# Batch 3's up product by Strassen's scheme, with joins on VectorE and copies on ScalarE

## The chip, the core and the metric

The kernel runs on one core of a Trainium2 chip. The metric is the time of one execution on the device, in microseconds (us). PE is the tensor engine, PEld its weight load, DVE the vector engine, ACT the scalar engine, POOL GpSimd, SP the engine that issues most of the transfers.

## What is computed

Attention with a few global and a window of local keys, then a low-rank mix over the sequence and a channel MLP with residual:

```python
# q, k, v: (4, 8, 768, 64); U: (768, 32); V: (32, 768); w_ch1: (512, 2048); w_ch2: (2048, 512)
scores = q @ k.T / 8 + bias            # 8 global keys, 96 local ones, a slope for each head
a = softmax(where(keep, scores, -1e9))
x = (a @ v) -> (4, 768, 512)           # heads side by side
h = x.T @ U @ V
u = x + h.T
out = u + relu(u @ w_ch1) @ w_ch2      # float32
```

`u @ w_ch1` is called the up product here, the product with `w_ch2` the down product.

## The kernel before, in words

The work is cut into 16 pairs of heads; pair i is heads 2(i % 4) and 2(i % 4) + 1 of batch i // 4. For each pair q and k are loaded and cast to fp16, transposed (by PE, from pair 7 on by transposing transfers, `turn`, L295), scored in `visit` (L352), scaled with the bias on DVE (`st_S`, L364), exponentiated on ACT (`st_E`, L376), multiplied with v (`st_av`, L383) and normed on DVE (`st_norm`, L403). POOL casts the result to fp16 (`st_x16`, L415). The low-rank mix follows: `st_low` and `st_lt` (L428, L439; L419 for some pairs), `st_M3` (L448), whose result DVE adds to the fp32 x (`st_add`, L461, two instructions of 128x384). Then `st_C` (L499) casts the sum to fp16 on POOL, and `st_X` (L492) issues a transposing transfer on SP that writes a quarter of uT, the transposed u of the batch. Four such quarters make a batch's uT; the up product of a batch waits for pair 3, 7, 11 or 15 last.

The up product (`up_mm`, L512) makes one 128-row block of the hidden layer in a PSUM bank with four matmuls over the 512 channels. Its moving side is a group of tokens: 384 and 384 for batches 0 and 1, 512 and 256 for batches 2 and 3 (`TG`, L65). So batches 2 and 3 have 16 blocks of four 512-column matmuls and 16 of four 256-column ones each. ACT takes each block out with a ReLU (`up_relu`, L526) into one of two tiles, htr0 and htr1.

The down product of batches 0 and 1 is plain (`down_mm`, L529). That of batches 2 and 3 goes by Strassen's scheme in Winograd's form, two row blocks of 128 tokens at a time (a row pair): seven products of eight 256-column matmuls (`product`, L595) in the order 1, 5, 6, 2, 7, 4, 3 (`PRODUCTS`). Three PSUM banks A, B, C serve a row pair. Product 1 opens A, 6, 7 and 4 add to it; between them DVE takes the value of A out (`gather`, L611, "a" after product 1, "b" after 6, "c" after 7) and joins it with B and C to the four quarters of the output. The sums that the products 5, 6, 7, 3 need on the hidden side are four DVE instructions for a row pair, `h_sum` (L572), those on the weight side are made once (`w_sum`, L561).

The whole order is written down by a planner inside the kernel (L630 to the end). Each piece of work is a `Step` (L643) with its engine or a choice of engines, a cost in us, the steps it depends on, the number of PSUM banks it needs, and sometimes a due time (`pace(i)`, L729) or laziness. The planner keeps a clock for each engine and for the DMA bus, and issues the step that can start first. At each turn PE takes the first of these that is ready: an attention step, a plain down product, a Strassen product (`next_product`, L993; between up groups at the rate of `PACE`, L1039), an up group (`do_up`, L944). The instructions of an engine then run in exactly this order, each waiting for its own semaphores, so a step that comes later than the planner thought holds up all that stands behind it on its engine. `open_pair` (L956) makes the steps of one row pair when the up groups of its tokens are put.

Staging tiles are in rotating pools: `stp` (loaded q, k, v and their fp16 form), `kp`, `scp` (scores), `vap`, `xp` (x, fp16 x, uT), `ffp` (hidden and output). The h sums before lie in free slots of `stp` and `scp`, and every second output block in one of `stp`.

Of the kernel before, what the change touches and what calls it, by code (L numbers as in the profile page):

```python
# [11 lines left out]
FP32 = mybir.dt.float32  # L12
# [8 lines left out]
def kernel(  # L21
# [13 lines left out]
    nc = tc.nc  # L35
# [35 lines left out]
    stp = ctx.enter_context(tc.tile_pool(name="stp", bufs=2))  # L71
    kp = ctx.enter_context(tc.tile_pool(name="kp", bufs=2))
    scp = ctx.enter_context(tc.tile_pool(name="scp", bufs=2))
    vap = ctx.enter_context(tc.tile_pool(name="vap", bufs=2))
    xp = ctx.enter_context(tc.tile_pool(name="xp", bufs=2))
    ffp = ctx.enter_context(tc.tile_pool(name="ffp", bufs=2))
    psum = ctx.enter_context(tc.tile_pool(name="psum", bufs=1, space=bass.MemoryType.PSUM))

    banks = [psum.tile([P, 512], FP32, name=f"bank{j}") for j in range(8)]
# [381 lines left out]
    def st_add(i, g):  # L461
# [99 lines left out]
    def w_sum(k, part):  # L561
        cs = slice(part * HC // 2, (part + 1) * HC // 2)
        o, x, y = (t[:, cs] for t in WSUM[k])
        nc.vector.tensor_tensor(o, x, y, ALU.subtract)

    sums, accs = {}, {}

    def quarters(b, n):
        g, ts = group(b, n)
        return htrs[b, g][:, 0:HC, ts], htrs[b, g][:, HC:NJC, ts]  # L570

    def h_sum(b, n, k):  # L572
        if k in (1, 3):
            if n // 2 % 2 == 0:
                nm = "qst" if k == 1 else "kst"
                home = [
                    stp.tile([P, 2, NSB, D], FP32, name=nm, tag=nm, bufs=2)
                    .rearrange("p h n d -> p (h n d)").bitcast(FP16)[:, 0:HC * P]
                    for _ in range(2)
                ]  # L580
            else:
                nm = f"sp{k // 2}"
                t = scp.tile([P, W], FP32, name=nm, tag=nm, bufs=1).bitcast(FP16)
                home = [t[:, j * HC * P:(j + 1) * HC * P] for j in range(2)]
            for j in range(2):
                sums[b, n, (1, 2, 3, 4)[k - 1 + j]] = home[j].rearrange("p (c t) -> p c t", c=HC)
# [6 lines left out]
        nc.vector.tensor_tensor(S[k], x, y, op)  # L593

    def product(b, n, k):  # L595
        (a11, a12), (a21, a22) = quarters(b, n), quarters(b, n + 1)
# [8 lines left out]
        for c in range(HC):  # L605
# [2 lines left out]
                skip_group_check=not fresh,  # L608
            )

    def gather(b, n, k):  # L611
        acc, t, cs, fresh = {
            "a": ("A", n, lo, True), "b": ("A", n, hi_, True), "c": ("A", n + 1, hi_, True),
            "11": ("B", n, lo, False), "12": ("C", n, hi_, False), "22": ("C", n + 1, hi_, False),
            "21": ("A", n + 1, lo, True),
        }[k]
        if (b, t) not in osbs:
            if t == n:
                osbs[b, t] = ffp.tile([P, DM], FP32, name="osb", tag="osb", bufs=3)
            else:  # L620
                osbs[b, t] = stp.tile([P, 2 * NSB, D], FP32, name="vst", tag="vst", bufs=2).rearrange(
                    "p n d -> p (n d)")[:, 0:DM]
# [215 lines left out]
    def pair(i):  # L838
# [36 lines left out]
        else:  # L875
# [4 lines left out]
            free_of[u][0].first = lc  # L880
        m = add(("m3", i), "PE", 0.34, lambda: st_M3(i), [("tc", i)], banks=2)
        free_of[m] = [
            add(("add", i, g), "DVE", 0.55, lambda g=g: st_add(i, g), [("m3", i)])
            for g in range(2)
        ]
# [18 lines left out]
    for st in pe_todo + waiting:  # L904
# [8 lines left out]
    since, last_out = 0, deque()  # L913
    left = {(b, g): TG[b][g] for b in range(B) for g in range(2)}
    relus, prods, opened, wsums = {}, [], [], {}

# [38 lines left out]

    def open_pair(b, n):  # L956
        g = int(n >= TG[b][0])
        rel = [relus[b, g, j] for j in range(NJC)]
        before = opened[-2] if len(opened) > 1 else None
        homes = [before[k] for k in PRODUCTS] if before else [  # L960
            steps[k, NPAIR - 1, j] for k in ("cq", "e") for j in range(2)]
        stored = before["end"] if before else [steps["cv", NPAIR - 1]]
        me = {}
        for k, deps in ((3, rel), (1, rel), (2, []), (4, [])):
            me["S", k] = other("DVE", 0.7, lambda k=k: h_sum(b, n, k), deps + homes + [
                me["S", j] for j in {2: (1,), 4: (3, 2)}.get(k, ())])
        for k in PRODUCTS:
            me[k] = Step("PE", 0.872, lambda k=k: product(b, n, k), rel, banks=int(k in "125"))
            me[k].nm = ("Q", b, n, k)
        for k, src in ("a", "1"), ("b", "6"), ("c", "7"), ("21", "4"), ("11", "2"), ("22", "5"), ("12", "3"):  # L970
            me["G", k] = other("DVE", 0.43, lambda k=k: gather(b, n, k), [me[src]] + stored)
# [17 lines left out]
        me["free"] = {"1": [me["G", "21"]], "5": [me["G", "12"]], "2": [me["G", "11"]]}  # L989
        opened.append(me)  # L990
        prods.append((b, n, me, list(PRODUCTS)))

    def next_product(now):  # L993
        for b, n, me, todo in sorted(prods[:2], key=lambda p: 0 if ups_q else -len(p[3])):
# [22 lines left out]
    def do_down():  # L1017
        if not begun:
            b, n = downs_q.popleft()
            parts = [  # L1020
                Step("PE", 0.87 if b or j else 1.08, lambda j=j: down_mm(b, n, j), banks=(j == 0))
                for j in range(NJC // 4)
            ]
            for p in parts:
                p.nm = ("D", b, n)
            ev = other("DVE", 0.65, lambda: down_add(b, n), parts[-1:] + list(last_out)[:1])
            if len(last_out) == 3:
                last_out.popleft()
            last_out.append(other("SP", 0.55, lambda: down_out(b, n), [ev], move=0.8))
            begun.extend(parts)  # L1030
            left[b, int(n >= TG[b][0])] -= 1
            put(begun.popleft(), [ev])
        else:
            put(begun.popleft())
            if not begun and not downs_q:
                sum_weights((2, 3))

    UP, RELU = 0.2165, 0.0865
    PACE = {(2, 1): 1, (3, 0): 2, (3, 1): 2}  # L1039
    begun, after, filled, lately = deque(), 0, 0, 0  # L1040
    while pe_todo or ups_q or downs_q or begun or prods:
        now = clock["PE"]
        drain(now)
        room = free_banks()[0][0]
# [5 lines left out]
        if not (after and down <= now):  # L1050
# [1 line left out]
                p for p in pe_todo if p.start() <= now + 0.05  # L1052
                and (p.banks != 2 or now < 31 or free_banks()[2][0] <= now + 0.5)
            ), None)
        prod = next_product(now)
        if step is not None:
            pe_todo.remove(step)
            put(step, free_of.get(step, ()))
# [1 line left out]
        elif down <= now + 0.05 and (begun or since >= 5 or after or up > now):  # L1060
            since = since if begun else max(0, since - 5)
            do_down()
            after = max(0, after - 1)
        elif prod and (lately >= PACE[ups_q[0][:2]] if up <= now + 0.05 else True):
            do_product(*prod)
            lately = 0
        elif up <= now + 0.05:
            b, g, _ = ups_q[0]
            do_up()
            since, after, lately = since + UP * TG[b][g] / 0.65, 0, lately + 1  # L1070
        else:
            soon = [p.start() for p in pe_todo + waiting] + [up, down]
            soon += [me[k].start() for _, _, me, todo in prods[:2] for k in todo]
            clock["PE"] = max(min(soon), now + 0.05)
            if 8 < now < 30 and clock["PE"] < math.inf:
                filled += 0.8 * (clock["PE"] - now) / 0.056
# [42 lines left out]
```

## Time and profile before

| | us |
|---|---|
| runs (3) | 224.8, 225.51, 226.29; median 225.51 |
| the profiled execution's own time | 225.93 |
| span of its profile | 223.0 |
| PE busy | 217.3 |
| DVE, ACT, POOL busy | 154.3, 115.0, 83.4 |

The page gives busy times of the engines, 40 slices of the span with the busy share in tenths, the chain of work that ended last (each step followed back to what released it), and groups of instructions by line. "PE 92%" in the chain means that for 92% of the span the end was set by PE's own work. In groups and timelines a PE instruction has its pipeline's fill in it, so that a row of eight 256-column matmuls shows 1.04 us and is followed by the next row 0.87 us after its start.

### The profile page before, as it was taken

To read this page: it belongs to the slowest core of one execution; us is meant where nothing else is said; L and a number is where in the kernel's file an instruction comes from. 1 tells how busy PE (TensorE), PEld (TensorE's weight loads), DVE (VectorE), ACT (ScalarE), POOL (GpSimd) and SP (SyncE) were. 2 spreads that over 40 slices of the span, in tenths; PEclk is the share of its full clock that TensorE was granted. 3 is DMA by queue.
4 is the path that set the end of the run, shared out by engine and by line. 5 is a ranking of instruction groups with operands and counts; after the bars stand their busy time and mean duration, and the time that the engine had idled before them with its cause. 6 is when DMAs were issued, how large, how long until landed. Compare 5 with 4: busy or idle time off the path is not lost.

```text
span 223.0 us, 5373 instructions
## 1 busy us (share of the span) xinstructions
PE 217.3 (97%) x2144; PEld 143.9 (65%) x2147; DVE 154.3 (69%) x349; ACT 115.0 (52%) x201; POOL 83.4 (37%) x125
## 2 busy tenths in 40 slices
PE   7999999999999998999999999999999999999994
PEld 3665876666565555655566555556988656688883
DVE  5768739576779595979977798797876702274662
ACT  5788576986464026664487040969224244444100
POOL 6646795605635653382624726322210000000000
PEclk9999999999999999999999999999999999999999
DMA  6999999999889998979799999710110400200204
GB/s 183 317 324 203 318 229 252 215 197 215 194 227 196 246 241 180 233 148 240 155 215 172 222 178 257 160 38 0 38 35 3 188 0 3 94 0 3 94 24 165
DMA packets 88871, 35.69 MB, mean 160 GB/s; under 512 B 78320, under 2 KB 85520, under 8 KB 88848
## 3 DMA queue, kind: packets, MB, share of 16 engines
q1 hardware_dynamic: 84320, 31.07, 59.1%
q0 software_dynamic: 4528, 4.29, 11.8%
q8 instruction: 16, 0.26, 0.5%
q14 instruction: 7, 0.06, 0.1%
HBM read 27.46 MB, written 6.29 MB: 151 GB/s over the span
## 4 chain that ended last, share of the span: by engine, by line
PE 92%; DMA 4%; DVE 2%; issue 1%; POOL 0%; DVEq 0%; POOLq 0%
PE bank L519 37%; PE bank L539 17%; PE bank L606 16%; PE bank L359 4%; PE bank L393 3%; PE bank L234 3%; DMA uT<-x 2%; PE bank L389 2%; PE bank L316 2%; PE bank L323 2%; PE bank L454 2%; PE bank L152 2%; DMA qst<-in_q_dram 1%; PE bank L431 1%; PE bank L423 1%; PE bank L478 1%
## 5 line engine op out<-in xcount | busy, mean ns | idle before, releaser
L519 PE MATMUL bank<-uT,w 128*128 128x384 f16 (+2 forms) x512 | 92.9, 326 | 0.8 <-DMA uT<-x 0.8
L527 ACT ACTIVATE htr<-bank 128x384 f16<-128x384 f32 (+2 forms) x128 | 60.1, 491 | 56.0 <-PE bank L519 53.4
L519 PEld LDWEIGHTS <-w 128*128 128x128 f16 x512 | 47.9, 98 | 28.3 <-issue 1.0
L378 ACT ACTIVATE ep<-sp 128x1408 f16<-128x1408 f32 x24 | 33.0, 1373 | 26.5 <-DVE sp L370 26.1
L539 PE MATMUL bank<-w,htr 128*128 128x512 f16 x192 | 45.8, 379 | 0.0
L370 DVE SCALAR_TENSOR_TENSOR sp<-bank,relcat 128x512 f32<-128x512 f32 (+1 forms) x72 | 41.2, 637 | 3.5 <-PE bank L359 3.3
L539 PEld LDWEIGHTS <-htr 128*128 128x128 f16 x192 | 17.5, 98 | 17.9
L417 POOL CAST x<-x_sb 128x384 f16<-128x384 f32 x30 | 17.2, 577 | 31.1 <-DVE x_sb L413 31.1
L127 POOL CAST v<-vst 128x768 f16<-128x768 f32 x16 | 13.8, 864 | 19.1 <-DMA vst<-in_v_dram 17.4
L501 POOL CAST x<-x_sb 128x768 f16<-128x768 f32 x12 | 10.3, 861 | 19.3 <-DVE x_sb L464 15.4
L413 DVE TENSOR_TENSOR x_sb<-bank,rcp 128x384 f32<-128x384 f32 x30 | 16.7, 558 | 1.0
L606 PEld LDWEIGHTS <-htr 128*128 128x128 f16 x144 | 14.0, 98 | 2.2
L393 PE MATMUL bank<-v,ep 128*128 128x65 f16 x192 | 15.5, 193 | 0.0
L393 PEld LDWEIGHTS <-ep 128*128 128x128 f16 x192 | 13.6, 98 | 2.3
L464 DVE TENSOR_TENSOR x_sb<-bank,x_sb 128x384 f32<-128x384 f32 x24 | 12.3, 552 | 3.6 <-PE bank L454 2.5
L389 PE MATMUL bank<-vA,ep 128*128 128x65 f16 x160 | 13.8, 194 | 0.0
L343 ACT ACTIVATE ep<-bank 128x512 f16<-128x512 f32 (+1 forms) x24 | 11.7, 576 | 2.4 <-PE bank L323 1.4
L406 DVE RECIPROCAL rcp<-bank 128x6 f32<-128x6 f32 x32 | 6.1, 191 | 9.2 <-PE bank L393 8.6
L606 PE MATMUL bank<-w,htr 128*128 128x256 f16 x96 | 12.1, 273 | 0.0
L389 PEld LDWEIGHTS <-ep 128*128 128x128 f16 x160 | 10.9, 97 | 1.8
L284 POOL COPY vA<-v 128x650 f16<-128x650 f16 x16 | 11.7, 731 | 0.9
L624 DVE TENSOR_TENSOR osb<-bank,x_sb 128x256 f32<-128x256 f32 x12 | 5.1, 422 | 9.5 <-PE bank L606 9.5
(109 smaller groups left out, 292.9 us busy)
## 6 DMA issues: line engine op xcount, KB each, us to landing
qst<-in_q_dram SPq DMA_DIRECT2D x16, 384.0 KB, 5.5
kst<-in_k_dram SPq DMA_DIRECT2D x16, 384.0 KB, 5.8
vst<-in_v_dram SPq DMA_DIRECT2D x16, 384.0 KB, 5.4
out_dram<-osb SPq DMA_DIRECT2D x17, 256.0 KB, 2.7
w<-in_moe_w_ch_dram POOLq DMA_DIRECT2D x6, 512.0 KB, 10.2
out_dram<-vst SPq DMA_DIRECT2D x5, 256.0 KB, 2.0
w<-in_moe_w_ch_dram POOLq DMA_DIRECT2D x1, 1024.0 KB, 10.7
out_dram<-osb SPq DMA_DIRECT2D x2, 128.0 KB, 1.7
```

The lines of the kernel that those rows point to most:

```text
L127: nc.gpsimd.tensor_copy(vt.rearrange("p n h d -> p h n d")[:, :, :, 0:D], vsts.pop(i).rearrange("p (h n) d -> p h n d", h=2),)
L370: nc.vector.scalar_tensor_tensor(out=sps[i, hi][:, c0:c0 + tot], in0=raw.pop((i, hi, c))[:, 0:tot], scalar=qk_scale / slope[2 * (i % NP) + ...
L378: nc.scalar.activation(ep, sps.pop((i, hi)), AF.Exp, scale=slope[2 * (i % NP) + hi])
L389: nc.tensor.matmul(ob[:, qi], ep[:, OF[qi - 1]:OF[qi - 1] + P], vA[:, qi - 1, hi], start=True, stop=False,)
L393: nc.tensor.matmul(ob[:, qi], ep[:, DG[qi]:DG[qi] + P], vt[:, qi, hi], start=(qi == 0), stop=True,)
L413: nc.vector.tensor_tensor(xo, ob[:, :, 0:D], rb, ALU.mult)
L417: nc.gpsimd.tensor_copy(x16, xo)
L464: nc.vector.tensor_tensor(dst, ups3.pop((i, g))[:, 0:GT].rearrange("p (t d) -> p t d", t=NTG), dst, ALU.add)
L519: nc.tensor.matmul(hps[:, 0:cols], w1_16[:, dc, jt * P:(jt + 1) * P], uTs[b][:, dc, c0:c0 + cols], start=(dc == 0), stop=(dc == NDC - 1),)
L527: nc.scalar.activation(htrs[b, g][:, jt], hps_t.pop((b, g, jt))[:, 0:TG[b][g] * P], AF.Relu)
L539: nc.tensor.matmul(cps, htr[:, jc, ts], w2_16[:, jc], start=(b > 0 and jc == 0), stop=(jc == NJC - 1),)
L606: nc.tensor.matmul(accs[b, n, acc], x[:, c], y[:, c], start=(fresh and c == 0), stop=(c == HC - 1), skip_group_check=not fresh,)
```

## The change

The up product of batch 3 is no longer made by `up_mm`. It goes by Strassen's scheme over the whole batch: w_ch1 and uT are quartered (256 channels by 1024 hidden rows, 256 channels by 384 tokens), and for each of 8 hidden blocks j seven products of two 384-column matmuls are made, 56 products in all. Where the scheme takes a value of bank A out, ACT copies it into an SBUF tile ("cut"), DVE joins it with bank B or C into the tile `hidden` (fp16), ACT takes the last quarter out with a ReLU, and the other three quarters get their ReLU in SBUF, on ACT or POOL. At most two blocks j are open at a time. The weight sums (8 instructions of 128x1024) and the four sums of u may go to DVE or POOL, and so may the h sums of the down product; the planner decided for POOL in all weight sums and 11 of 24 h sums. For these tiles the attention's pools (`stp`, `kp`, `scp`, `vap`) are closed after the last pair and a new pool `last` takes their memory; the h sums of batch 2 therefore begin only then.

For pairs 7 and 15, DVE writes the fp16 x itself (`st_add16`, two instructions, out of PSUM and the fp32 x), before the two adds that update the fp32 x, and the transfer `st_X` waits for these two. POOL's cast `st_C` is left out for them.

The planner's loop gets the new products (`next_quad`, at most six in a row while another product or up group is ready), and with other steps its order moves elsewhere too: in the stretch of batch 1's up product the visits of pairs 8 to 11 and their low-rank steps stand at other places, and around the end of attention batch 2's down products come later. The total of PE's other work is the same.

The core of the diff:

```diff
+    def st_add16(i, g):
+        b, dc = i // NP, i % NP
+        ts = slice(NTG * g, NTG * (g + 1))
+        nc.vector.tensor_tensor(
+            x16s[b][:, dc, ts], ups3[i, g][:, 0:GT].rearrange("p (t d) -> p t d", t=NTG),
+            xs[b][:, ts, dc * P:(dc + 1) * P], ALU.add,
+        )
...
-        nc.vector.tensor_tensor(S[k], x, y, op)
+        eng.tensor_tensor(S[k], x, y, op)
...
+    def up_product(j, k):
+        b11, b12, b21, b22 = u_quarters()
+        x, y, acc, fresh = {
+            "1": (a11w, b11, "A", True), "2": (a12w, b21, "B", True),
+            "3": (upw.get(4), b22, "C", False), "4": (a22w, usum.get(4), "A", False),
+            "5": (upw.get(1), usum.get(1), "C", True), "6": (upw.get(2), usum.get(2), "A", False),
+            "7": (upw.get(3), usum.get(3), "A", False),
+        }[k]
+        if fresh:
+            qacc[j, acc] = bank()[:, 0:GT]
+        for c in range(2):
+            nc.tensor.matmul(
+                qacc[j, acc], x[:, c, j * P:(j + 1) * P], y[:, c], start=(fresh and c == 0),
+                stop=(c == 1), skip_group_check=not fresh,
+            )
+
+    def up_cut(j, k):
+        cuts[j, k] = last_pool().tile([P, GT], FP32, name=f"cut{k}", tag=f"cut{k}", bufs=2)
+        nc.scalar.copy(cuts[j, k], qacc[j, "A"])
+
+    def up_join(j, k):
+        acc, cut, row, cs = {
+            "11": ("B", "a", j, slice(0, GT)), "12": ("C", "b", j, slice(GT, S)),
+            "22": ("C", "c", j + HC, slice(GT, S)),
+        }[k]
+        nc.vector.tensor_tensor(late["h"][:, row, cs], qacc[j, acc], cuts.pop((j, cut)), ALU.add)
+
+    def up_last(j):
+        nc.scalar.activation(late["h"][:, j + HC, 0:GT], qacc[j, "A"], AF.Relu)
+
+    def up_floor(j, k, eng):
+        t = late["h"][:, j] if k == "11" else late["h"][:, j + HC, GT:S]
+        if eng is nc.scalar:
+            eng.activation(t, t, AF.Relu)
+        else:
+            eng.tensor_scalar_max(t, t, 0.0)
...
+        if i in (NPE - 1, NPAIR - 1):
+            halves = [("half", i, g) for g in range(2)]
+            for g in range(2):
+                add(halves[g], "DVE", 0.55, lambda g=g: st_add16(i, g), [("m3", i)])
+            add(("xt", i), "SP", 1.2, lambda: st_X(i), halves + [("read", b - 2)], move=0.3)
+            return
...
-        (b, g, jt) for b in range(B) for lo in range(0, NJC, 4 if b == 0 else NJC)
+        (b, g, jt) for b in range(B - 1) for lo in range(0, NJC, 4 if b == 0 else NJC)
...
-            me["S", k] = other("DVE", 0.7, lambda k=k: h_sum(b, n, k), deps + homes + [
+            me["S", k] = other(SUM, 0, lambda e, k=k: h_sum(b, n, k, e), deps + homes + [
...
+    RATIO = 6
+    SUM = (("DVE", 0.7), ("POOL", 2.3))
+    gone = [steps["n", i, hi] for i in (NPAIR - 2, NPAIR - 1) for hi in range(2)]
...
+    def sum_up_weights():
+        for k in (1, 2, 4, 3):
+            for part in range(2):
+                deps = [last_add[0]] + (gone if k == 3 else [])
+                deps += [sumsof["w", j, part] for j in {2: (1,), 4: (2,)}.get(k, ())]
+                sumsof["w", k, part] = other(
+                    SUM, 0, lambda e, k=k, part=part: up_w_sum(k, part, e), deps, lazy=0.8)
...
-        prod = next_product(now)
+        prod, quad = next_product(now), next_quad(now)
...
+        elif quad and not (mixed >= RATIO and (prod or up <= now + 0.05)):
+            do_quad(*quad)
+            mixed += 1
```

In the changed kernel the lines are: `st_add16` L481, `st_add` L474, `w_sum` L582, `h_sum` L607, `product` L620, `up_w_sum` L645, `u_sum` L659, `up_product` L672, `up_cut` L679, `up_join` L686, `up_last` L689, `up_floor` L694 and L696, `gather` L712, `up_mm` L537.

More of the change, by code (lines that the diff above doesn't have):

```diff
@@ L559, with w_sum, h_sum @@
             (T4, wB[:, :, lo], T2), (T3, wB[:, :, hi_], wA[:, :, hi_])]
-    def w_sum(k, part):
+    def w_sum(k, part, eng=nc.vector):
         cs = slice(part * HC // 2, (part + 1) * HC // 2)
         o, x, y = (t[:, cs] for t in WSUM[k])
-        nc.vector.tensor_tensor(o, x, y, ALU.subtract)
+        eng.tensor_tensor(o, x, y, ALU.subtract)
     sums, accs = {}, {}
     def quarters(b, n):
+        if b == B - 1:
+            ts = slice(n * P, (n + 1) * P)
+            return late["h"][:, 0:HC, ts], late["h"][:, HC:NJC, ts]
         g, ts = group(b, n)
         return htrs[b, g][:, 0:HC, ts], htrs[b, g][:, HC:NJC, ts]
[L572 to L580, printed above, removed]
-            else:
[L582 to L586, printed above, removed]
+    def h_sum(b, n, k, eng):
+        if k == 3:
+            if (b, n) == (B - 1, NSB - 2):
+                t = upw["all"].rearrange("p (j c t) -> p j c t", j=6, c=HC)
+            else:
+                t = last_pool().tile([P, 4, HC, P], FP16, name="hsum", tag="hsum", bufs=2)
+            for j in range(4):
+                sums[b, n, j + 1] = t[:, j]
         (a11, a12), (a21, a22) = quarters(b, n), quarters(b, n + 1)
@@ L609, in product, with up_w_sum @@
             )
+    JQ = DFF // 2
+    a11w, a12w, a21w, a22w = (
+        w1_16[:, r:r + 2, c:c + JQ] for c in (0, JQ) for r in (0, 2)
+    )
+    usum, upw, cuts, qacc = {}, {}, {}, {}
+    def up_w_sum(k, part, eng):
+        if k == 3:
+            if part == 0:
+                upw[3] = last_pool().tile([P, 2, JQ], FP16, name="usum3")
+        elif not upw:
+            t = xp.tile([P, NSB, DM], FP32, name="x_sb", tag="x_sb", bufs=3)
+            t = t.rearrange("p n d -> p (n d)").bitcast(FP16)
+            upw["all"] = t
+            for j, kk in enumerate((1, 2, 4)):
+                upw[kk] = t[:, j * 2 * JQ:(j + 1) * 2 * JQ].rearrange("p (c n) -> p c n", c=2)
+        x, y, op = {
+            1: (a21w, a22w, ALU.add), 2: (upw.get(1), a11w, ALU.subtract),
+            3: (a11w, a21w, ALU.subtract), 4: (a12w, upw.get(2), ALU.subtract),
+        }[k]
+        eng.tensor_tensor(upw[k][:, part], x[:, part], y[:, part], op)
@@ new lines, in u_quarters, with u_sum @@
+    def u_quarters():
+        u = uTs[B - 1]
+        return [u[:, r:r + 2, c:c + GT] for r in (0, 2) for c in (0, GT)]
+    def u_sum(k, eng):
+        if k == 1:
+            t = xp.tile([P, NP, NSB, P], FP16, name="x16", tag="x16").rearrange("p c n d -> p (c n d)")
+            usum["all"] = t
+            for j in range(4):
+                usum[j + 1] = t[:, j * 2 * GT:(j + 1) * 2 * GT].rearrange("p (c n) -> p c n", c=2)
+        b11, b12, b21, b22 = u_quarters()
+        x, y = {1: (b12, b11), 2: (b22, usum.get(1)), 3: (b22, b12), 4: (b21, usum.get(2))}[k]
+        eng.tensor_tensor(usum[k], x, y, ALU.subtract)
@@ L970, in open_pair @@
         for k, src in ("a", "1"), ("b", "6"), ("c", "7"), ("21", "4"), ("11", "2"), ("22", "5"), ("12", "3"):
[L971 removed]
+            me["G", k] = other("DVE", 0.43, lambda k=k: gather(b, n, k), [me[src]] + (stored if k in ("c", "21") else first_stored))
         for k, after in (("11", "a"), ("22", "c"), ("12", "b")):
@@ new lines, with next_quad, do_quad @@
+    late_chain = steps["add", NPAIR - 1, 1]
+    def next_quad(now):
+        for me in [q for q in quads if q["todo"]][:2]:
+            for k in me["todo"]:
+                if me[k].start() <= now + 0.05:
+                    return me, k
+                if k in "125":
+                    break
+        return None
+    def do_quad(me, k):
+        put(me[k], me["free"].get(k, ()))
+        me["todo"].remove(k)
+        if not any(q["todo"] for q in quads):
+            for n in range(0, NSB, 2):
+                open_pair(B - 1, n)
@@ L995, in next_product @@
+    def next_product(now):
+        if any(0 < len(q["todo"]) < len(PRODUCTS) for q in quads):
+            open_now = prods[:1]
+        else:
+            open_now = prods[:3]
+        for b, n, me, todo in sorted(open_now, key=lambda p: 0 if ups_q else -len(p[3])):
             for k in todo:
@@ L1036, in do_down @@
                 sum_weights((2, 3))
+                sum_up_weights()
     UP, RELU = 0.2165, 0.0865
     PACE = {(2, 1): 1, (3, 0): 2, (3, 1): 2}
-    begun, after, filled, lately = deque(), 0, 0, 0
-    while pe_todo or ups_q or downs_q or begun or prods:
+    begun, after, filled, lately, mixed = deque(), 0, 0, 0, 0
+    while pe_todo or ups_q or downs_q or begun or prods or any(q["todo"] for q in quads):
         now = clock["PE"]
@@ L1073 @@
             soon += [me[k].start() for _, _, me, todo in prods[:2] for k in todo]
+            soon += [q[k].start() for q in quads for k in q["todo"]]
             clock["PE"] = max(min(soon), now + 0.05)
```

79 lines of the change are left out of this document (64 added, 15 removed).

## The prediction

> **What bounds the kernel now.** I read the page's busy shares and slices first, then the chain that ended last, then what PE waited for.
>
> ```profile
> PE 217.3 (97%) x2144; PEld 143.9 (65%) x2147; DVE 154.3 (69%) x349; ACT 115.0 (52%) x201; POOL 83.4 (37%) x125
> PE   7999999999999998999999999999999999999994
> POOL 6646795605635653382624726322210000000000
> PEclk9999999999999999999999999999999999999999
> PE 92%; DMA 4%; DVE 2%; issue 1%; POOL 0%; DVEq 0%; POOLq 0%
> ```
>
> TensorE bounds it: 97% busy at the full granted clock, 92% of the chain. The others have room, POOL above all: nothing after some 164 us. So time is won by fewer PE columns or by a PE wait removed, and lost by any new PE wait. Among PE's waits after the start only one is large:
>
> ```profile
> PE bank L519 <- DMA uT<-x: 0.8, 1, 0.8
> ```
>
> The chain around it: batch 1's up product starts when pair 7's transposed x has landed.
>
> ```profile
> 78.76 0.56 DVE x_sb L464
> 79.44 0.83 POOL x L501
> 80.45 4.79 DMA uT<-x
> 85.28 0.97 PE bank L519 x5
> ```
>
> The second add ends at 79.32, POOL's cast follows, the transfer is issued at 80.45.
>
> Unit prices of PE, from the timeline of PE (start, then the busy time with the pipeline's fill; the step to the next start is the price):
>
> ```profile
> 174.48 1.89 PE L519 MATMUL bank<-uT,w 128*128 128x512 f16 x8
> 176.21 1.04 PE L606 MATMUL bank<-w,htr 128*128 128x256 f16 x8
> ...
> 204.89 1.04 PE L519 MATMUL bank<-uT,w 128*128 128x256 f16 x8
> 205.76 1.04 PE L606 MATMUL bank<-w,kst 128*128 128x256 f16 x8
> ```
>
> and from the chain, where no fill is counted, 384 columns: 3.25 / 20 = 0.1625 us each.
>
> ```profile
> 94.14 3.25 PE bank L519 x20
> ```
>
> **The change, part by part.** The profiled execution took 225.93 us: span 223.0 and 2.93 around it. The median of the runs is 225.51, 0.42 lower.
>
> *PE work.* Removed: batch 3's 32 up groups, 64 matmuls of 512 columns (8 in 1.73 us: 13.84) and 64 of 256 (8 in 0.87: 6.96), 20.8 us. Added: 56 products of two 384-column matmuls, 112 x 0.1625 = 18.2. Gain 2.6 us, all on the bound engine. The weight loads (98 ns) still fit under 162 ns. The 42 down products keep their number and price (0.87 each); six of batch 2's that stood among its own up groups now come after batch 3's up products have begun, which moves the begin of these from 174.5 to about 163, with 5.2 us less cover for pair 15's chain.
>
> *fp16 x of pairs 7 and 15.* Two DVE instructions, like L464 (0.55 each), write fp16 x at once, before the two adds; POOL's cast is gone and the transfer waits on DVE. DVE has 2.2 us more in all. For pair 7 the transfer goes out right behind the second instruction, some 79.4 instead of 80.45, and on SP's queue it now stands ahead of an output write (0.36 us) that preceded it. It would land at 84.2. In the new order PE reaches the fourth up matmul at about 84.0, as one attention product is moved behind. So 0.6 of the 0.76 us is gained (0 if the transfer takes longer, 0.76 at best). What is late next is still this transfer.
>
> *ACT.* 32 ReLUs out of PSUM (16 x 0.60 and 16 x 0.38, 15.7 us) become 24 copies and 8 last ReLUs of 128x384 (0.49 by L527's mean): 15.7. Ten ReLUs in SBUF on ACT, 7 x 0.49 and 3 x 0.83 (as L179's 128x768), add 5.9. That is 21.6 us in a stretch of some 26, for which PE waits by link: product 1, copy, product 6, copy, product 7, copy, product 4. With two blocks in flight and a down product after about six, the tightest copy ends 0.1 to 0.2 us before its product's turn. Bounds 0 to 1 us; I take 0.
>
> *DVE.* 24 joins of 128x384 (0.55, as L464), 4 sums of u (128x768; by L593's 0.685 for 1024, 0.51), minus 11 of 24 h sums now on POOL: 13.2 + 2.1 - 7.5 = 7.8 us more. In the busy times by stretch DVE works 20.9 of the 45.3 us from 174.5 to 219.8, so they fit. After the last join a ReLU must be done for batch 3's first product 1, and sums for its first product 5: three down products (2.6 us) cover the one, twelve (10.5 us) the other. I take 0; the tightest sum, for the third row pair's product 5, is 0.3 us early, so up to 1 us if DVE runs late.
>
> *POOL and the one wait I expect.* POOL gets 8 weight sums and 11 h sums of 128x1024 with two inputs, and 6 ReLUs in SBUF. The first sums stand among the last attention casts: behind them queue fp16 x of pairs 14 and 15, for which PE's low-rank products wait. Then POOL goes on without a gap: after pair 15's last cast come five sums, and the fifth is what batch 2's first product 5 needs (the first tiles in the closed pools' memory wait on transfers long landed: 0). No row has a two-input POOL instruction. The casts give 0.51 for 384 and 0.83 for 768 elements: 0.19 + 0.83 us per 1024 to 1.02, so one input read costs 1.04 for 1024. Bounds: 1.04, if the second input is free, and 2.2, twice a whole cast scaled (0.83 x 1024/768 x 2). I take 1.9, two reads with one start: 0.19 + 2 x 0.853. [...]
>
> To that comes DVE's hold on POOL:
>
> ```profile
> 142.99 0.51 POOL L417 CAST x<-x_sb 128x384 f16<-128x384 f32 x1
> ...
> 146.90 0.90 POOL L417 CAST x<-x_sb 128x384 f16<-128x384 f32 x1 [1.21 <-DVE x_sb L413]
> 153.32 1.03 POOL L417 CAST x<-x_sb 128x384 f16<-128x384 f32 x1 [5.52 <-DVE x_sb L413]
> 155.65 1.15 POOL L501 CAST x<-x_sb 128x768 f16<-128x768 f32 x1 [1.29 <-DVE x_sb L464]
> 157.09 0.90 POOL L417 CAST x<-x_sb 128x384 f16<-128x384 f32 x1 [0.29 <-DVE x_sb L413]
> ```
>
> ```profile
> 155.43 0.68 DVE L593 TENSOR_TENSOR kst<-htr 128x1024 f16<-128x1024 f16 x1
> 156.94 0.68 DVE L593 TENSOR_TENSOR qst<-htr 128x1024 f16<-128x1024 f16 x1
> ```
>
> A cast that meets a DVE sum of two SBUF tiles grows: 0.46 us of overlap costs 0.32, 0.53 costs 0.39, so 0.7 of the overlap; DVE keeps its 0.68. [...]
>
> Now POOL against PE, from pair 15's last cast to product 5. POOL: 5 x 1.9 = 9.5; DVE has six such sums in that stretch, three of weights (0.68) and three of u (0.51): 0.7 x 3.57 = 2.5; together 12.0. PE: low-rank group 0.15, down product 0.87, transpose 0.06, 12 up groups x 0.436 = 5.23, M3 0.33, ten up products x 0.325 = 3.25: 9.9. The cast ends some 0.2 us before PE comes to the low-rank group (0.7 in the trace: 157.99 to 158.66; POOL's sums take the rest). PE itself waits 0.3 on the way: pair 15's transfer leaves 1.2 us after M3 and takes 3.5 (median of L494), then two sums of u come before product 6: 5.7 to 6.2 us, against 5.9 of PE work. Wait: 12.0 - 9.9 - 0.2 - 0.3 = 1.6. Bounds: 0 (5.2 + 2.5 is under 9.9) and 4 (2.2 each and the overlap lost whole: 11 + 3.6 = 14.6, less 10.4). The later POOL sums keep 0.7 us or more to their products.
>
> *End.* The last three row pairs go in turn instead of two; the last add (0.42) and the last 128 KB write stay: 0.
>
> *Sum.* 225.93 - 2.6 - 0.6 + 0.3 + 1.6 = 224.6 against the profiled execution's own time; 0.42 lower for the median of runs: 224.2.
>
> **The rivals.** A: POOL is in time. If its sum costs 1.04 to 1.6 us, or DVE's hold is milder, only the 0.3 remains: 225.51 - 3.2 + 0.3 = 222.6. For it: POOL has a gap of 1.2 us or more before three of the four casts shown. Against it: the lengthened casts.
>
> B, slower: POOL becomes the bound around the hand-over. At 2.2 us for a sum and the whole overlap lost, pair 15's cast itself comes 0.6 to 0.8 us late for the low-rank group, and product 5 waits 4: 225.51 - 3.2 + 0.3 + 0.7 + 4.0 = 227.3. It turns slower than before when these waits pass 2.9 us: with 0.7 of the overlap lost, that is at about 2.15 us for a sum. For it: the rows of lengthened casts. Against it: no row has a sum so dear.
>
> C: the new order in batch 1 costs a wait. The planner puts pair 10's scores some 4 us earlier against the clock of before, and its transposed q and k come by DMA in a stretch where the page's DMA row stands at 8 and 9 tenths. POOL's casts for them ended at 84.6, transfers take about 3, so 94 us should do; if not, 1 to 2 us on top of the sum: 225.7.
>
> That the change does not do what it says is hardly open: PE's columns fall by 64 x 768 - 112 x 384 = 6144, and rows price all three widths.
>
> **How the numbers follow.** Forecast (waits of about 1 to 3 us in all) 0.38; A 0.30; B 0.22; C 0.10. The time is the likeliest's, 224.2, its own range 223.2 to 225.4. The range over the cases: 222.4 (A) to 227.0 (most of B). A measurement of this kernel tells about 1%, 2.26 us, from no change: under 223.25 is faster, over 227.77 slower. Faster: A whole and a little of the forecast, 0.32; slower: a third of B and a little of C, 0.10; the rest, 0.58, within 1%.
>
> **What would show it.** Up products of batch 3 about 0.325 us apart, 18.2 in sum. No PE wait on uT near 84 us, or under 0.3. A POOL sum at 1.9 us, growing beside DVE's L582 and L659. One PE wait of 1 to 2 us on POOL's hsum at the first product 5 of batch 2. Wrong, if PE waits on ACT's copies inside the up products, if POOL's sums cost over 2.1 or under 1.6 us, or if PE waits before 150 us.

## The result, and the profile after

The changed kernel takes 233.83 us (median of 6 runs, 232.48 to 235.57), the kernel before 225.41 (6 runs): a ratio of 1.0377, 95% interval 1.0339 to 1.0415. It is slower by 8.4 us, where 224.2 was predicted. The profiled execution took 232.48, with a span of 230.7 (223.0 before).

From the page of the changed kernel (busy time, PE, POOL and PE's clock in 40 slices of 5.8 us, the chain by engine):

```profile
PE 217.4 (94%) x2131; PEld 142.2 (62%) x2131; DVE 175.9 (76%) x370; ACT 118.9 (52%) x211; POOL 135.3 (59%) x148
PE   7999999999999999999999999999569999978994
POOL 6548792616635710766456269899964999923000
PEclk9999999999999999999999999999979999999999
PE 71%; DVE 9%; POOL 8%; DMA 4%; issue 4%; ACT 1%; SPq 0%; DVEq 0%
```

PE is as busy as before in us, in a longer span: what is new is idle time. It lies in one place (slices 29 and 30, 161 to 173 us, with the clock down in the second) and in smaller holes from 202 us. PE's waits (what, on what; sum, times, longest):

```profile
PE bank L672 <- DVE x L659: 4.7, 1, 4.7
PE bank L620 <- DVE osb L712: 1.3, 1, 1.3
PE bank L620 <- DVE hsum L607: 0.9, 1, 0.9
PE bank L620 <- POOL hsum L607: 0.5, 1, 0.5
```

The wait for uT at batch 1 is gone, and no wait over 0.2 us stands between 60 us and 163.6, where batch 3's up products begin (product 1 of the first two blocks). Then PE stands still for 4.7 us, for a u sum on DVE. DVE's and POOL's timelines there (start, duration, count; several in one line run back to back):

```profile
161.72 4.89 DVE L582 TENSOR_TENSOR w<-w 128x1024 f16<-128x1024 f16 x2
166.54 4.86 DVE L659 TENSOR_TENSOR x<-uT 128x768 f16<-128x768 f16 x2
171.32 0.55 DVE L659 TENSOR_TENSOR x<-uT,x 128x768 f16<-128x768 f16 x1
```

```profile
158.89 4.66 POOL L645 TENSOR_TENSOR usum<-w 128x1024 f16<-128x1024 f16 x2
163.50 7.48 POOL L607 TENSOR_TENSOR hsum<-htr 128x1024 f16<-128x1024 f16 x3
```

DVE is not idle in the profile: each of the four sums in the first two rows is itself 2.4 to 2.6 us long while POOL runs its sums without a gap, and a sum takes 0.55 as soon as POOL is done (170.98). A hold inside an instruction shows here as a longer instruction, not as a wait. POOL's sums are 2.12 us alone and up to 2.6 there: the two alternate, and each of the four DVE sums ends 0.42 to 0.55 us after one of POOL's. The tiles differ, save in the first of them (DVE on `w` and `uT`, POOL on `htr`), so it is no matter of the same data. Behind the idle time PE ran slowly (windows: length, PE busy and matmuls, clock, DMA share, GB/s; and its timeline):

```profile
166.00:169.00 3.00, 0.00 (x0) 0.97 0.00 0
169.00:172.00 3.00, 2.82 (x9) 0.50 0.00 0
172.00:175.00 3.00, 2.76 (x18) 0.96 0.00 0
```

```profile
169.68 0.85 PE L672 MATMUL bank<-uT,w 128*128 128x384 f16 x2
170.31 0.85 PE L672 MATMUL bank<-x,x_sb 128*128 128x384 f16 x2
...
175.03 0.49 PE L672 MATMUL bank<-uT,x_sb 128*128 128x384 f16 x2
175.35 0.49 PE L672 MATMUL bank<-x,w 128*128 128x384 f16 x2
```

Products stand 0.63 us apart at half clock and 0.32 to 0.33 later, as predicted. Batch 2's first product 5 comes at 173.83; by work alone it would have come at 166.83. Of the 10.4 us that PE loses from 163.6 on (its time there less the price of its products), 7.0 are lost here.

### The profile page after: what moved, and what is told of

The parts are those of the page before. It is cut to its first block, busy times and chain, and to the rows that moved or that the text cites. A ratio compares the mean times of both kernels' runs of the same rounds, so it can differ in the third digit from the quotient of the medians.

```text
span 230.7 us, 5411 instructions
## 1 busy us (share of the span) xinstructions
PE 217.4 (94%) x2131; PEld 142.2 (62%) x2131; DVE 175.9 (76%) x370; ACT 118.9 (52%) x211; POOL 135.3 (59%) x148
## 4 chain that ended last, share of the span: by engine, by line
PE 71%; DVE 9%; POOL 8%; DMA 4%; issue 4%; ACT 1%; SPq 0%; DVEq 0%
PE bank L537 25%; PE bank L557 16%; PE bank L620 10%; POOL hidden L696 4%; POOL hsum L607 4%; PE bank L369 3%; DMA qst<-in_q_dram 3%; PE bank L403 3%; PE bank L399 2%; PE bank L672 2%; DVE w L582 2%; PE bank L326 2%; PE bank L244 2%; PE bank L464 2%; DMA kst<-in_k_dram 2%
## 5 line engine op out<-in xcount | busy, mean ns | idle before, releaser
L537 PE MATMUL bank<-uT,w 128*128 128x384 f16 (+2 forms) x384 | 68.6, 326 | 0.1
L545 ACT ACTIVATE htr<-bank 128x384 f16<-128x384 f32 (+2 forms) x96 | 44.5, 491 | 28.6 <-PE bank L537 26.6
L537 PEld LDWEIGHTS <-w 128*128 128x128 f16 x384 | 35.5, 98 | 20.9 <-issue 0.2
L557 PEld LDWEIGHTS <-htr 128*128 128x128 f16 x192 | 17.4, 98 | 17.8
L620 PEld LDWEIGHTS <-hsum 128*128 128x128 f16 x160 | 15.5, 98 | 6.0 <-issue 1.5
L137 POOL CAST v<-vst 128x768 f16<-128x768 f32 x16 | 13.7, 858 | 8.3 <-DMA vst<-in_v_dram 8.2
L519 POOL CAST x<-x_sb 128x768 f16<-128x768 f32 x10 | 8.4, 838 | 15.1 <-DVE x_sb L474 9.5
L696 POOL TENSOR_SCALAR hidden<-hidden 128x768 f16<-128x768 f16 (+1 forms) x6 | 12.2, 2045 | 5.6 <-DVE hidden L686 5.6
L403 PEld LDWEIGHTS <-ep 128*128 128x128 f16 x192 | 13.5, 98 | 2.3
L474 DVE TENSOR_TENSOR x_sb<-bank,x_sb 128x384 f32<-128x384 f32 x24 | 12.4, 548 | 3.1 <-PE bank L464 2.4
L672 PE MATMUL bank<-x,x_sb 128*128 128x384 f16 x32 | 8.5, 356 | 4.8 <-DVE x L659 4.7
L712 DVE TENSOR_TENSOR osb<-bank,x_sb 128x256 f32<-128x256 f32 x22 | 9.1, 419 | 4.1 <-PE bank L620 3.3
```

Source lines behind the costliest of these rows:

```text
L137: nc.gpsimd.tensor_copy(vt.rearrange("p n h d -> p h n d")[:, :, :, 0:D], vsts.pop(i).rearrange("p (h n) d -> p h n d", h=2),)
L403: nc.tensor.matmul(ob[:, qi], ep[:, DG[qi]:DG[qi] + P], vt[:, qi, hi], start=(qi == 0), stop=True,)
L537: nc.tensor.matmul(hps[:, 0:cols], w1_16[:, dc, jt * P:(jt + 1) * P], uTs[b][:, dc, c0:c0 + cols], start=(dc == 0), stop=(dc == NDC - 1),)
L545: nc.scalar.activation(htrs[b, g][:, jt], hps_t.pop((b, g, jt))[:, 0:TG[b][g] * P], AF.Relu)
L557: nc.tensor.matmul(cps, htr[:, jc, ts], w2_16[:, jc], start=(b > 0 and jc == 0), stop=(jc == NJC - 1),)
L620: nc.tensor.matmul(accs[b, n, acc], x[:, c], y[:, c], start=(fresh and c == 0), stop=(c == HC - 1), skip_group_check=not fresh,)
```

## The experiments

Theory: while POOL runs an instruction that reads SBUF, a DVE sum with two SBUF inputs is held until it ends, so POOL's dense sums make DVE's u sums late. Rivals: the u sums are late by DVE's order or by pair 15's transfer; POOL's slow ReLUs did it; the scheme's own copies and joins cost it. All ratios are to the kernel before, run on the same chip, with 95% intervals. The diffs are shortened.

**All sums on DVE, in their places** (`e1_sums_dve`)

```
- eng.tensor_tensor(S[k], x, y, op)        # L607; L645 and L659 alike
+ nc.vector.tensor_tensor(S[k], x, y, op)
```

> The changed kernel with its order of emission kept, but every sum that it gave to POOL (8 weight sums, 11 h sums) issued on VectorE instead, at the same place of the order; all else alike. Theory 1 (POOL's two-input SBUF sums hold VectorE's two-input SBUF sums, and the PE waits come from that): the sums run at 0.55 to 0.70 us each, the 4.7 us PE wait before the first up product 5 goes, the clock stays near full, and the 10.4 us that TensorE lost behind batch 3's start shrink to 1 or 2: 223 to 226 us. Rival (order and transfer: the u sums are late because they stand behind L582 or because pair 15's transfer lands late): the wait of 4.7 us stays and the time is 231 or more. Rival (the up product in 56 small products with its copies and joins is itself the cost): stays over 230.

Measured: 225.34 us, ratio 0.9987 (0.9959 to 1.0015). PE's waits from 140 us on:

```profile
PE bank L672 <- ACT cuta L679: 0.3, 1, 0.3
PE bank L672 <- ACT cutb L679: 0.2, 1, 0.2
```

The last weight sum of the down product (L582) and the first u sums (L659) on DVE:

```profile
165.03 0.68 DVE L582 TENSOR_TENSOR w<-w 128x1024 f16<-128x1024 f16 x1
165.64 1.02 DVE L659 TENSOR_TENSOR x<-uT 128x768 f16<-128x768 f16 x2
```

All the loss goes with POOL's sums, though DVE has 19 sums more. The u sums still stand behind L582: order and transfer fall. So does a cost of the scheme that would explain 8 us.

**POOL copies in place of its sums** (`e2_one_input`)

```
+ if eng is nc.gpsimd: eng.tensor_copy(o, x)
+ else: eng.tensor_tensor(o, x, y, op)
```

> The changed kernel, but each sum that POOL does there is replaced by a POOL copy of the sum's first operand alone into the same place (the second operand is left out, so the outputs are not the reference's); what VectorE does is unchanged. It splits theory 1: if the hold is a matter of POOL's two-input instructions alone, VectorE's L582 and L659 sums that lie beside POOL's copies take 0.68 and 0.54 us, and the time is 223 to 226 us. If any POOL instruction on SBUF holds VectorE's two-input sums, they still take as long as the copy they meet (1 to 2 us), the wait at the first up product 5 halves rather than goes, and the time is 227 to 231. Rival (order and transfer): the wait stays at 4.7 and the time over 231.

Measured: 224.38 us, 0.9941 (0.9903 to 0.9978).

```profile
162.62 2.50 DVE L582 TENSOR_TENSOR w<-w 128x1024 f16<-128x1024 f16 x2
```

POOL's copies take 1.04 us alone, and the L582 pair 1.29 each instead of 2.48: the hold is there, and shorter with the shorter instruction. L582's rows are those of the second reading, the time is that of the first (223 to 226): the wait for a u sum is gone, not halved.

**POOL sums and POOL copies added to the kernel before** (`e4_before_pool_sums`, `e5_before_pool_copies`)

```
  nc.vector.tensor_tensor(S[k], x, y, op)          # L593, batch 3
+ nc.gpsimd.tensor_tensor(spare, a21, a22, ALU.add)   # e4
+ nc.gpsimd.tensor_copy(spare, a21); nc.gpsimd.tensor_copy(spare, a22)   # e5
```

> The kernel before, with one thing added: beside each of the 12 h sums of batch 3 on VectorE, POOL also adds two quarters of the hidden tensor into a spare tile that nobody reads. No other engine waits for POOL there. Theory 1: the POOL sums take about 2.1 us each, and VectorE's L593 sums that lie beside them go from 0.68 us to 1.3 to 2.7; TensorE waits for them at products 5 and 6, and the time rises by 2 to 9 us, to 227 to 234. If the two engines do not exclude each other (rival: POOL's sums were late only for those who read them), L593 keeps 0.68 and the time stays at 225.5, within 1.

> The control of the run before it: the kernel before, with two one-input POOL copies of the same quarters into the same spare tile in the place of each added sum. If only two-input POOL instructions hold VectorE's sums, L593 keeps 0.68 us and the time stays at 225.5, within 1. If every POOL instruction on SBUF does, L593 rises to 1 to 2 us and the time to 226.5 to 232.

Measured: 237.13 us, 1.0483 (1.0401 to 1.0566), with the sums; 228.81, 1.0159 (1.011 to 1.0208), with the copies. With the sums, DVE and then POOL:

```profile
195.54 0.69 DVE L593 TENSOR_TENSOR qst<-htr 128x1024 f16<-128x1024 f16 x1 [1.33 <-ACT htr L527]
197.00 1.76 DVE L593 TENSOR_TENSOR qst<-qst,htr 128x1024 f16<-128x1024 f16 x1
198.69 2.60 DVE L593 TENSOR_TENSOR sp<-htr 128x1024 f16<-128x1024 f16 x1
```

```profile
195.59 2.62 POOL L598 TENSOR_TENSOR ep<-htr 128x1024 f16<-128x1024 f16 x1 [31.82 <-ACT htr L527]
198.29 2.45 POOL L598 TENSOR_TENSOR ep<-htr 128x1024 f16<-128x1024 f16 x1
```

The pattern is plain here. The first DVE sum began 0.05 us ahead of POOL's: it kept 0.69, and POOL's took 0.5 more. The second began while POOL ran: it ended at 198.76, 0.55 after POOL's (198.21). The third ended at 201.29, 0.55 after POOL's second (200.74). In these rows the one that began first ran, and the other waited for its end. With the copies (1.38 and 1.39 us there) the same holds end 0.53 and 0.54 us after a copy's end (DVE, then POOL):

```profile
197.21 1.52 DVE L593 TENSOR_TENSOR sp<-htr 128x1024 f16<-128x1024 f16 x1
198.65 1.52 DVE L593 TENSOR_TENSOR kst<-htr,qst 128x1024 f16<-128x1024 f16 x1
```

```profile
198.25 1.38 POOL L599 COPY ep<-htr 128x1024 f16<-128x1024 f16 x1
```

The page's busy time of POOL is equal in the two (112.5 and 112.6 us), yet PE waits 7.4 us beside the sums and 1.1 beside the copies; most of the copies' 3.1 us is POOL's own tail, which runs on to 224.5, 3.0 past the last add. The time with the sums is over the 234 that I expected: from within a wait of 4.0 us on the clock stood at 0.50 from 205.5 to 215.5 us (0.77 on the mean of 200 to 210 us, 0.72 of 210 to 220), so PE's work took longer too. In both, DVE's adds that read PSUM and one SBUF tile (L629, L630) keep 0.42 us.

**Only the h sums, only the weight sums moved** (`e6_h_sums_dve`, `e7_weight_sums_dve`: L607, or L645 and L659, as in the first diff)

> The changed kernel with its order of emission kept, but the 11 h sums that it gave to POOL issued on VectorE; the 8 weight sums stay on POOL. Theory (VectorE's two-input sums wait out whatever POOL instruction on SBUF they meet): POOL has only the weight sums, which end near 163.5 us, so of the sums at the hand-over only the L582 pair is held, by 1 to 2 us; the u sums take 0.55 us each and the wait before the first up product 5 shrinks from 4.7 us to under 1.5. Against the run with all sums on VectorE (225.3) the 0.8 us that VectorE's weight sums cost ahead of batch 3 come back: 223 to 225.5. If it is the weight sums that do the harm, it stays over 229.

> The opposite half: the 8 weight sums on VectorE, the 11 h sums left on POOL. Theory: POOL's h sums still begin where batch 2's second hidden half is complete and run back to back beside the u sums, so these still take 1.5 to 2.5 us each and TensorE waits 2 to 5 us at the first up product 5, and the clock falls after it; the holds at 201 and 210 us stay too: 228 to 233. If the weight sums did the harm, 223 to 226.

Measured: 225.18 us, 0.999 (0.9961 to 1.002), with the h sums moved; 232.48, 1.029 (1.025 to 1.0331), with the weight sums moved. The h sums on POOL do nearly all the harm. In the second run the place was not the one expected: the u sums are 0.55 there, and PE waits 2.7 us ahead of them, up to 167.3, for pair 15's add (L474), which stands on DVE behind two held sums (L582 2.47 us, L645 2.14). So other DVE sums are held here than in the changed kernel (the L582 pair and two of L659, 2.4 to 2.6 us): those that stand beside POOL's.

**PE kept busy through its wait** (`e8_fill`)

```
+ if (j, k) == (0, "5"):
+     for _ in range(28):
+         nc.tensor.matmul(qacc[j, acc], w1_16[:, 0, 0:P], w1_16[:, 0, 0:GT], start=True, stop=True)
```

> The changed kernel with 28 matmuls of 384 columns added ahead of the first up product 5, on weights already there and into that product's own bank, which the product then clears; they read and delay nothing that VectorE or POOL waits for. They fill the 4.7 us in which TensorE stood still. If the idle time is what halves the clock behind it, the granted clock stays at 1.0 in 169 to 172 us, the up products there come 0.33 us apart, and the time falls by 1.5 to 2 us, to 231.5 to 232.5. If the clock falls for another reason, the products stay 0.63 apart and the time is 233.5 to 235.

Measured: 232.99 us, 1.0326 (1.0289 to 1.0363): 0.8 less, which the intervals do not separate from the changed kernel. The clock is 1.00 from 169 to 175 us (0.50 from 169 to 172 without the added matmuls) and the products stand 0.32 to 0.33 apart, so it was the idle time that halved it. The gain is under what I expected because product 6 meets the next late u sum:

```profile
PE bank L675 <- DVE x L659: 1.4, 1, 1.4
```

**The second part of the change alone** (`e9_fp16_only`: `st_add16` and its steps for pairs 7 and 15, on the kernel before)

> The kernel before with only the second part of the change: the fp16 x of pairs 7 and 15 by VectorE straight from PSUM. By the prediction the 0.76 us wait for uT at batch 1's first up product goes and 0.3 may be lost at pair 15: minus 0.3 to minus 0.8, so 224.7 to 225.3. If the wait is only moved, no change.

Measured: 226.37 us, 1.0029 (1.0005 to 1.0053). No gain; if anything it is 0.3% slower, outside the 224.7 to 225.3 that I expected. The 0.8 us wait for uT becomes three of 0.2 (uT, ACT's `htr`, the weight sum L572). In the other runs with this edit the wait for uT was between nothing and 0.6.

**POOL's ReLUs on ACT; the u sums ahead of L582** (`e10_relu_act`, `e11_u_first`)

```
- else: eng.tensor_scalar_max(t, t, 0.0)       # e10, L696
+ nc.scalar.activation(t, t, AF.Relu)
```

In `e11_u_first` the last two L582 sums are issued behind the third u sum.

> The changed kernel with its order of emission kept, but the ReLUs over finished rows of the hidden tensor that it gave to POOL (2.0 us each there on the mean, where the sum had 0.83) issued on ScalarE (0.85 and 0.52 us). Rival (POOL's slow ReLU, not its sums, is what made the tail late): the waits of TensorE at 201 and 210 us and the late h sums go, and the time falls by 2 to 4 us, to 230 to 232. Theory: the 4.7 us at the first up product 5 lie ahead of the first ReLU and stay; in the tail the POOL sums come earlier but hold VectorE's sums as before: 232 to 234.5.

> The changed kernel with one thing moved: VectorE's last two weight sums of the down product (L582, 162 to 166.5 us) stand behind the first three u sums instead of ahead of them; POOL has all its work. Rival (the u sums are late because they stand behind L582 in VectorE's order): they run at 0.55 us each from 162 us, the 4.7 us go, and the time is 223.5 to 226. Theory: moving them changes who is held, not that someone is: each of the three meets a POOL sum and takes 1.5 to 2.5 us; the first is done near 164.5, so product 5 is in time, but product 6 needs the third and waits 2 to 4 us for it; the tail is as before: 229 to 232.

Measured: 233.9 us, 1.0363 (1.0305 to 1.042), and 233.47, 1.0331 (1.0263 to 1.04): neither helps. Without the ReLUs POOL's sums only follow more closely: the wait on POOL's h sum is gone, but PE waits 6.7 us in all for u sums (4.7 and 2.0). With the u sums first, product 5 comes in time and product 6 waits 3.1 us; I had expected the time to fall more (229 to 232), but the next wait (1.4 us, for a join behind the held L582) and the clock took it, which stood at 0.50 from 171.5 to 178 us (products 0.64 us apart).

**A version after these runs** (`e12_best`, then `e13_no_pool_beside` and `e16_order`) **and a finer cut** (`e14_quarters`: each POOL sum in four instructions of 256 columns)

> A version after what the runs showed: all h sums and u sums on VectorE; of the weight sums of the up product six on POOL, done ahead of the hand-over, and two on VectorE from 168 us on; the L582 pair behind the u sums; the planner is given the measured 2.15 and 1.2 us for POOL's ReLUs, and so puts most of them on ScalarE. Theory: no POOL instruction lies beside the sums of the hand-over; of the waits only those on ScalarE's copies at the first up products stay (1 to 2 us), so most of the 2.6 us of columns is left: 223 to 224.5, against 225.5 before. If Strassen's up product costs as much in copies and joins as it saves, 225 to 226.5.

Measured: 245.67 us, 1.0888 (1.0829 to 1.0948), a plain miss. Given new costs, the planner put pair 15's value cast (L137) behind the weight sums on POOL, at 157.8 us; pair 15's x came 5 us later (its M3 group at 165.0; 160.0 in the run with the ReLUs moved), and batch 2's h sums too: PE waits 6.8 us for these. So the next versions keep the order and move single sums.

> The changed kernel with its order of emission kept but for this: h sums on VectorE; six of the eight weight sums of the up product stay on POOL; the last two go to VectorE, and with the L582 pair they stand behind the first three u sums. Theory: no POOL sum lies beside the hand-over; the wait of 0.8 us for the u sum that the run with h sums alone moved (225.2) still had goes, and only waits on ScalarE's copies at the first up products stay: 223.5 to 225, a gain of 0.2 to 0.9% on the kernel before. If the loss that was left there is the scheme's own (copies and joins that one pair of quads waits for), no gain: 225 to 226.

> The changed kernel, but every sum on POOL is cut into four instructions of 256 columns; the work and its order are the same. If VectorE's sum is held until POOL's running instruction ends and then goes ahead, the hold falls from about 1.9 us to under 0.7, the u sums take 0.6 to 1.3 us, and the wait of 4.7 us falls under 2, though POOL's sums grow to 2.3 to 2.8 us by the fixed part of each instruction: 227 to 231. If VectorE has to wait until POOL's whole run of sums is over, or if the rates only share, the u sums take 2 us or more as before, and the time is 233 to 236.

Measured: ratio 1.0019 (0.9982 to 1.0056) for the first, and 232.72 us, 1.0305 (1.0253 to 1.0357), for the quarters. In the quartered run the u sums take 0.72 to 1.02 us, the first up product 5 comes 0.25 us late and product 6 waits 0.4: here too the hold ends with POOL's running instruction. But a POOL sum in four parts is 2.6 us long alone and up to 4.0 beside DVE's sums, and now PE waits for POOL itself, so that the time is above the 227 to 231 expected for this case:

```profile
PE bank L635 <- POOL hsum L590: 2.7, 4, 2.0
PE bank L635 <- DVE osb L727: 1.4, 1, 1.4
PE bank L635 <- POOL hidden L711: 0.8, 1, 0.8
```

In `e13_no_pool_beside` every DVE sum of the hand-over is 0.55 to 0.69, and PE still waits 2.2 us, for an h sum far back in DVE's queue. `e16_order` moves that sum ahead:

> The version with no POOL sum beside the hand-over, with VectorE's order mended at the one wait that it showed (2.2 us, for the h sum that the first product 5 of batch 2 reads): that h sum goes right behind the up product's last weight sums, ahead of the first joins, and the L582 pair behind the joins of the first two quads. Theory (in the hand-over VectorE's queue is the bound, not the copies): the wait falls under 0.5 us, and of the 2.6 us of columns 1.5 to 2 come out: 223.3 to 224.8, 0.4 to 1% under the kernel before. If the joins that now stand later make a wait of the same size (VectorE simply has too much work between the last x and the first products), no gain: 225 to 226.5.

Measured: 225.58 us, 1.0003 (0.9972 to 1.0034). The wait moves on and shrinks:

```profile
PE bank L633 <- DVE hsum L620: 0.9, 1, 0.9
PE bank L693 <- ACT cutb L700: 0.2, 1, 0.2
```

In PE's timeline of this run, the steps between products that are longer than their width's 0.325 or 0.87 add up to some 2.3 us between 164 and 193 us: 1.06 at that wait, the rest in steps of 0.06 to 0.41 behind copies and joins. In `e1_sums_dve` the same sum is 1.7 us, with the copies for sums 1.2. That is much of the 2.6 us of columns; that these steps are where the gain went is argued from them, and no run takes them away. No version beat the kernel before by more than the measurement can tell; only the one with copies for sums, which leaves out the second operand, did (0.6%).

## Why the prediction was wrong

- *PE work: right.* At the full clock products stand 0.325 us apart, 56 x 0.325 = 18.2; by these steps PE's work fell by 2.6 us.
- *fp16 x: the mechanism right, the size doubtful.* Pair 7's transfer goes out at 79.41 (79.4 predicted) and that wait is gone in the changed kernel. Alone, the edit gained nothing in the time (1.0029), so the 0.6 us is not borne out. The 0.3 us for pair 15 did not show as a wait.
- *POOL's price: too low, inside the bounds.* A sum is 2.12 us, not 1.9 (up to 2.6 beside DVE), over the 2.1 that the prediction named as a sign of being wrong. (In its working, 0.83 us per 1024 elements should be 0.853, which it then uses.) Its upper bound, 2.2 us from two whole casts, was nearer than that. POOL's ReLU of 128x768, which the prediction gave no price of its own (the 0.83 of an expectation above is a cast's), is 2.13; one of them stands ahead of the h sum for which PE waits 0.5 us at 180.5.
- *The one wait expected, for POOL's fifth sum: there, but hidden.* That sum ended at 168.6 us, 11.8 after pair 15's last cast (12.0 predicted) and 1.8 after the 166.83 at which product 5 would have come by work alone (1.6 predicted). PE's longer wait for DVE covered it.
- *The step that failed: "DVE keeps its 0.68", with DVE at 0 (bounds 0 to 1).* In the kernel before a cast of 128x384 takes 0.51 us beside L464 and L370, which read PSUM and one SBUF tile, and 0.90 to 1.03 beside L564 and L593, which read two. The step was read from such lengthened casts; they had begun 0.2 us or less into a DVE sum, so POOL waited. I read who had begun first as a rank of the engines. The kernel before already had the other side: behind the cast shown at 146.90, which ended at 147.80, a second DVE sum had begun at 147.35, and it ended 0.54 us after the cast:

```profile
147.35 0.99 DVE L564 TENSOR_TENSOR wsum<-w,wsum 128x1024 f16<-128x1024 f16 x1
```

In the changed kernel a POOL sum had begun ahead of each of DVE's four sums at the hand-over, and each took 2.4 to 2.6 us: 7.3 us more on DVE than their price (9.75 less 2 x 0.68 and 2 x 0.55). Three of the four stand before the first up product 5 and all four before product 6, and PE waited 4.7 us at the first of these, not, as predicted, at batch 2's product 5 for POOL's h sum. In all DVE's busy time rose by 21.6 us, where the prediction's 7.8 and 2.2 make 10.0; the rest is about the size of the holds. The runs that show it: with POOL's sums gone the wait goes (225.3); with POOL sums added to the kernel before, PE waits behind DVE's held sums there too (237.1).

- *Both sides stand in one run.* In `e4_before_pool_sums`, with two SBUF inputs on both engines, the DVE sum that began first took 0.69 us, and those that did not ended 0.55 us after POOL's end.
- *Rival B was the right side, the wrong place.* It had POOL late for PE and 227.3 us; the lateness was DVE's, and the one wait went beyond the 4 us that it allowed. Rival C did not come: no wait over 0.2 us in its stretch.
- *ACT at 0 to 1: right within the changed kernel (0.2 us of waits).* With POOL's sums out of the way PE's lengthened steps add up to 1.7 (`e1_sums_dve`) to 2.3 us (`e16_order`), behind copies, joins and late sums together. So the change, as its order stands, would have gained next to nothing even without the holds: 0.9987 (0.9959 to 1.0015) in `e1_sums_dve`.
- *End at 0: wrong.* The waits that end at 204.2 and 213.2 us (1.3 and 0.9) stand behind DVE h sums of 2.60 and 2.41 us, which began at 201.3 and 210.1 and were held in the same way.

## What to carry to other kernels

Before work is moved from DVE to POOL, look for DVE instructions with two SBUF inputs beside it: each may have to sit out the POOL instruction it meets, and in these traces that shows as a longer DVE instruction (2.4 to 2.6 us for 0.55 or 0.68) and not as a wait. Read a lengthened row together with who began first; a row that shows one order says nothing of the other. And columns saved on a full TensorE count only as far as the chains that feed the shorter products are shorter too: here small waits for copies, joins and sums took 1.7 to 2.3 us of the 2.6.

## What the runs showed of the hardware

- A POOL copy of one fp16 tile (1.04 us for 128x1024) holds a DVE sum too (0.68 becomes up to 1.52 us in `e5_before_pool_copies`), not only a two-input POOL instruction (up to 2.60 us in `e4_before_pool_sums`). The hold ends with the running POOL instruction (the DVE sum ends 0.55 us after it in `e4_before_pool_sums`); then DVE goes ahead of POOL's next (2.45 us there, 2.12 alone).
- A POOL ReLU in place on 128x768 fp16 takes 2.13 us in the changed kernel, twice a copy of 128x1024 (1.04 in `e5_before_pool_copies`).
- After a wait of 4.7 us the granted clock was 0.50 for about 3 us in the changed kernel (169 to 172 us); with dummy matmuls in the gap it stayed at 1.00 (`e8_fill`). It was halved behind shorter waits too: one of 2.7 us in `e7_weight_sums_dve` (0.50 from 167 to 170 us; matmuls of 256 columns 0.21 us apart, 0.109 at the full clock) and one of 3.1 us in `e11_u_first` (0.50 from 171.5 us, 1.7 after it; products 0.64 us apart), while one of 2.2 us in `e13_no_pool_beside` left it at 1.00 (products 0.325 us apart).
